# A two-layer decode step: one head's output weights on half of the DMA engines, scores on all 32 rows of a block, and three more filler matmuls

## The chip, the cores and the metric

The kernel runs on one core of one Trainium2 chip. The metric is device time in microseconds. Before the change the runs took 711.59, 712.06 and 712.72 us; their median, 712.06 us, is the time before.

## The reference, cut to what matters

Four tokens (B = 4, one position each, D = 640) go through attention, an MLP, the same attention and the same MLP again. The weights and the caches of the two attention layers are the same arrays, and so are those of the two MLPs. Everything is float32.

```python
x = x + A(layernorm(x));  x = x + M(layernorm(x))     # round one
x = x + A(layernorm(x));  x = x + M(layernorm(x))     # round two

def A(x):                       # 32 heads of 128, the last 1024 positions of the cache
    q = (x @ wq).reshape(B, 1, 32, 128).transpose(0, 2, 1, 3)
    p = softmax(einsum("bhqd,bhkd->bhqk", q, k) * 128 ** -0.5)
    o = einsum("bhqk,bhkd->bhqd", p, v)
    return o.transpose(0, 2, 1, 3).reshape(B, 1, 4096) @ wo

def M(x):                       # D -> 1728 -> D
    return relu(x @ w1) @ w2
```

Keys and values differ per batch entry and per head, so almost nothing that is loaded is used more than four times, and one round reads about 150 MB.

## The kernel before, in words

**Data.** For each head a record of 9,472 columns on 128 rows lies in HBM: the head's part of wq (5 blocks of 128 columns), its keys for 4 batch entries (4,096 columns), its values (4,096 columns) and its part of wo (640 columns; a row is one of the head's 128 dimensions). On the chip, `store` has room for some five records, `ring` has 4,320 columns and `kept` the tail of one record. The MLP's weights lie in a second array and come through `ring` and a spare part of `store`.

**Rounds and heads.** A loop `for r in range(2)` (line 501) makes the two rounds; r is 0 in round one and 1 in round two. Round one takes heads 0 to 31. Its last five records stay in `store`, and round two begins with them. Inside a round the heads are pipelined (lines 514 to 539): in step n PE makes the scores of head n+1, the values of head n, and the query of head n+2, and then projects head n's output.

One head's work is:

- `query` (line 385): 5 matmuls of 128 by 128 weights give q for four batch entries; DVE scales it into `qT`.
- `scores` (line 398): for each half of the positions and each batch entry b one matmul of 512 columns. The weights are q of entry b, repeated; the result goes to rows 32b and following of a PSUM tile `sc_ps`. The repetition is 4, so rows 32b to 32b+3 hold the same scores and the other 28 rows of the block hold what was there before.
- `softmax` (line 413): DVE takes the maximum over each row, ACT the exponential over all 128 rows with the sum of each row to `tot`.
- `weights` (line 421): DVE brings the sum of each block's first row to all its 32 rows (a transpose of 32 columns to `spread`), takes the reciprocal, and multiplies it with the mask `of_batch` into a factor `mrt` for each row and batch entry. Then it transposes the exponentials in blocks of 32 by 32 and multiplies them by `mrt` into `wT`, from which PE reads them as weights.
- `values` (line 434): 8 matmuls; `picks` (line 444): DVE masks and sums the result; `output_T` (line 449): PE turns it, ACT copies it to `oTs`; `project` (line 454): 4 matmuls add the head's contribution to `acc`.

A float32 matmul stands in the profile as two instructions, so the 8 matmuls of a head's scores are 16 lines of PE.

**Late heads.** In round one the last six heads' wo pieces come after the keys and values of all heads, and are used at the round's end (lines 555 to 562).

**Order of the work.** Every engine runs its instructions in the order in which the program is written (class `InOrder`, line 88). All loads are issued by the queue of SP. They stand in a list `items` in a fixed order; `pump` (line 278) issues the next one as soon as its place on the chip is free, and never one ahead of another. `done` (line 300) tells that a piece has been used for the last time. `cols` (line 293) finds the columns of a loaded piece.

**Fillers.** `busy` (line 350) is a matmul whose result nobody reads; it keeps PE at work in places where it would wait. Four of them stand at the end of each round ahead of the last head's query (line 524).

**Who waits for whom at the end of round one.** The query of the last head waits for its record. The values of the last two heads wait for theirs, and the projections for the late wo pieces. Then the MLP starts with the weights that have come into `ring`, and each piece that it has used lets SP issue a further one, first of the MLP and then of round two's heads.

Of the kernel before, what the change touches and what calls it, by code (L numbers as in the profile page):

```python
# [32 lines left out]
F32 = mybir.dt.float32  # L33
AF = mybir.ActivationFunctionType
OP = mybir.AluOpType
# [3 lines left out]
P = 128  # L39
B, D, H, DH, W, FF = 4, 640, 32, 128, 1024, 1728  # L40
NB = 4
FD = D // NB
# [4 lines left out]
WQ, K, V, WO = 0, D, D + 4 * W, D + 8 * W  # L47
REC = 2 * D + 8 * W
# [11 lines left out]
KEPT = WO - 4 * 512  # L60
# [18 lines left out]
LATE = 6  # L79
# [2 lines left out]
FIVE = [REC + 6272, 2 * REC - 3072, 2 * REC - 3200]  # L82
LAST_FIVE = [REC + 4736, 2 * REC - 4736, REC, REC]
THREE = [REC + HALF, REC + HALF]
GROUPS = [{h: FIVE for h in range(0, 25, 5)}, {6: THREE, 9: FIVE, 14: FIVE, 19: LAST_FIVE}]


# [19 lines left out]


@with_exitstack
def decode_kernel(ctx: ExitStack, tc: tile.TileContext, xf, rec, wm, out):  # L110
    nc = tc.nc
    pe, dve, act, pool, sp = (InOrder(tc, e) for e in (nc.tensor, nc.vector, nc.scalar, nc.gpsimd, nc.sync))
    sb = ctx.enter_context(tc.tile_pool(name="sb", bufs=1))
# [4 lines left out]
    wT = scratch[:, :128].rearrange("p (i c j) -> p i c j", i=2, c=16)  # L118
# [4 lines left out]
    spread = scratch[:, 256:288]  # L123
    hT = scratch.rearrange("p (m j) -> p m j", j=32)
    oTs = sb.tile([P, LATE, B], F32, name="oTs")
    qT = sb.tile([P, B], F32, name="qT")
    of_batch = sb.tile([P, B], F32, name="of_batch")
    of_block = sb.tile([P, 4], F32, name="of_block")
    rows = sb.tile([P, 2 * B], F32, name="rows")
    pick, rrow = rows[:, :B], rows[:, B:]  # L130
    mrt = sb.tile([P, B], F32, name="mrt")
    small = sb.tile([P, 14], F32, name="small")
    nmax, rtot, rstd, eps, eps_dh, ones, unused, sums, tot0, tot1 = (small[:, i:i + 1] for i in range(10))
    squares = small[:, 10:]
    tot = [tot0, tot1]
    store = sb.tile([P, FIRST + NS * REC], F32, name="store")
    kept = sb.tile([P, REC - KEPT], F32, name="kept")
    ring = sb.tile([P, RING], F32, name="ring")

    sc_ps = [ps.tile([P, W], F32, name=f"sc_ps{i}") for i in range(2)]  # L140
    t_ps = ps.tile([P, 512], F32, name="t_ps")
    o_ps = ps.tile([P, 512], F32, name="o_ps")
    acc = ps.tile([P, 512], F32, name="acc")
# [30 lines left out]
    LAST = H - NS  # L174


    def home(h, r):

        if r:
            return FIRST + (h if h >= LAST else h - 6 + LAST) % NS * REC  # L180
        return (0 if h < NS else FIRST) + h % NS * REC

    items = []
# [4 lines left out]
    buffers = {"store": store, "ring": ring, "kept": kept}  # L188

    def load(src, lo, hi, buf, col, parts):  # L190
        items.append((src[:, lo:hi], buf, col, hi - lo, parts))

    def place(buf, col):
        return ("store", spare + FROM + col) if buf == "spare" else (buf, col)
# [6 lines left out]
    def run(r, lo, hi, buf, col):  # L201
        parts = [(("rec", r, h), max(lo - h * REC, 0), min(hi - h * REC, REC), col + max(h * REC - lo, 0))
                 for h in range(lo // REC, (hi - 1) // REC + 1)]
        load(rec, lo, hi, buf, col, parts)

    def piece(r, h, lo, hi, buf="store", col=None):
        run(r, h * REC + lo, h * REC + hi, buf, home(h, r) + lo if col is None else col)


    def group(r, h, sizes):  # L210
# [21 lines left out]
    for h in hs[:-3]:  # L232
        if h in GROUPS[0]:
            group(0, h, GROUPS[0][h])
        if h >= 25:
            piece(0, h, 0, KEPT if h == LAST - 1 else WO if h >= H - LATE else REC)
        if h == LAST - 1:
            piece(0, h, KEPT, WO, "kept", 0)
    ending(0, hs, True)
# [16 lines left out]
    c, end = new[1] * REC, new[6] * REC  # L256
    for buf, lo, hi in places:
        if lo == old[1]:
            piece(1, new[0], WO, REC, buf, lo)
        elif c < end:  # L260
            cut = max(x for x in cuts if x <= min(end, c + hi - lo))
            run(1, c, cut, buf, lo)
            c = cut
# [14 lines left out]
    def pump():  # L278

        while items:  # L280
            src, buf, col, n, parts = items[0]
            if any(b == buf and x < col + n and col < y for b, x, y in live):
                return
            sp.dma_start(buffers[buf][:, col:col + n], src)
            live.append((buf, col, col + n))
            for key, lo, hi, c in parts:
                at.setdefault(key, []).append((lo, hi, buf, c))
            items.pop(0)
# [1 line left out]
    def pieces(key):  # L290
        return at[key if key in at else (key[0], 0) + key[2:]]

    def cols(key, lo, n):

        for x, y, buf, col in pieces(key):
            if x <= lo and lo + n <= y:
                return buffers[buf][:, col + lo - x:col + lo - x + n]
        raise KeyError((key, lo, n))

    def done(key, lo, hi):  # L300

        if key[0] == "rec" and key[1] == 0 and key[2] >= LAST:
            return
        if key == ("rec", 0, 0):
            lo = max(lo, FIRST)
        for x, y, buf, col in pieces(key):
            free(buf, col + max(lo, x) - x, col + min(hi, y) - x)
        pump()
# [89 lines left out]
    def scores(r, h, s, first=False):  # L398
        key = ("rec", r, h)
        for i in range(2):  # L400
            for b in range(B):
                pe.matmul(sc_ps[s][32 * b:32 * b + 4, 512 * i:512 * i + 512], qT[:, b:b + 1].to_broadcast([P, 4]),
                          cols(key, K + 512 * (B * i + b), 512), start=True, stop=True)
            done(key, K + VH * i, K + VH * i + VH)
            if first and i == 0:
                if r:
                    unpark(0)
                deviation(eps_dh, float(DH), True)
                act.activation(unused, eps, AF.Exp)
                if r:  # L410
                    unpark(1)
# [8 lines left out]

    def weights(s, parts=((0, 2),)):
        if parts[0][0] == 0:

            dve.transpose(spread, tot[s].to_broadcast([P, 32]))
            dve.reciprocal(rtot, spread[:, 0:1])
            dve.tensor_scalar(mrt, of_batch, rtot, None, op0=OP.mult)
        for i, j in parts:
            w = sc_ps[s][:, 512 * i:512 * j]
            dve.transpose(w, w)
            dve.tensor_tensor(wT[:, i:j].rearrange("p i c j -> p (i c) j"),  # L430
                              w.rearrange("p (c j) -> p c j", j=32)[:, :, :B],
                              mrt.unsqueeze(1).to_broadcast([P, 16 * (j - i), B]), op=OP.mult)

    def values(r, h, last=False, fill=(0, 0)):
        key = ("rec", r, h)
# [10 lines left out]
        dve.tensor_tensor(o, o, of_block.unsqueeze(2).to_broadcast([P, 4, DH]), op=OP.mult)  # L446
        dve.tensor_reduce(on[last], o.rearrange("p c d -> p d c"), op=OP.add, axis=AX.X)

    def output_T(i, last=False, to=None):
        to = outs[last][:, :B] if to is None else to  # L450
        pe.matmul(to, on[last], pick, start=True, stop=True)
        act.copy(oTs[:, i], to)

    def project(r, h, i, end):
        key = ("rec", r, h)
        for n in range(NB):
            pe.matmul(acc[32 * n:32 * n + B, :FD], oTs[:, i], cols(key, WO + n * FD, FD),
                      start=False, stop=end, skip_group_check=True)
        done(key, WO, REC)
# [41 lines left out]
    for r in range(2):  # L501
        hs = order[r]
        late = LATE if r == 0 else 2
        center(384 * r, 128)
        query(r, hs[0], 0, True)
        if r:
            busy(192, warm)
        scores(r, hs[0], 0, True)
        softmax(0, (r, hs[1], 1))
        if r:  # L510
            unpark(2)
            unpark(3)
        weights(0, ((0, 1), (1, 2)))
        for n, h in enumerate(hs[:-2]):
            i = n - (H - late)
            s = (n + 1) % 2
            scores(r, hs[n + 1], s)
            if r and not n:
                busy()
            softmax(s)  # L520
            end = n == H - 3
            values(r, h)
            if end:
                for _ in range(4):
                    busy()
            picks(0)
            query(r, hs[n + 2], n + 2)
            if end:
                scores(r, hs[-1], 1)
                weights(s, ((0, 1),))  # L530
            if r and n < NS - 2:
                busy(320, sc_ps[n % 2])
            output_T(max(i, 0), to=None if r and not n else t_ps[:, :B])
            if r and not n:
                unpark(4)
            if i < 0:
                project(r, h, 0, False)
            if not end:
                weights(s)
        softmax(1)  # L540
        if not r:
            park(0)
            park(1)
        weights(0, ((1, 2),))
        values(r, hs[-2], 0, (0, 1))
        weights(1, ((0, 1), (1, 2)))
        picks(0)
        values(r, hs[-1], 1)
        if not r:
            park(2)  # L550
        output_T(late - 2)
        if not r:
            park(3)
        picks(1)
        for i in range(late - 3) if late > 2 else (0,):
            project(r, hs[H - late + i], i, False)
        if late == 2:
            busy()
        output_T(late - 1, True)
        dve.memset(pad, 0.0)  # L560
        for i in (late - 3, late - 1, late - 2) if late > 2 else (1,):
            project(r, hs[H - late + i], i, i == late - 2 or late == 2)
        center(256, 328)
        mlp(r)
# [39 lines left out]
```

## Time and profile before

| what | value |
|---|---|
| median of three runs | 712.06 us (711.59 to 712.72) |
| the profiled execution, first to last instruction | 710.7 us |
| TensorE busy | 502.4 us, 71% |
| VectorE busy | 317.4 us, 45% |
| ScalarE busy | 99.6 us, 14% |
| read from HBM | 301.34 MB |
| mean rate of all transfers | 425 GB/s |
| mean granted TensorE clock | 0.824 |

The profile is of one execution. Its own time is known as the span from its first to its last instruction, 710.7 us; the timed runs have 1.3 us more in the median, which lies ahead of the first or behind the last instruction.

How to read it: an engine's busy time says little here unless one asks for the stretch of the span. The page has a row of the DMA engines' busy share in 40 slices. The chain of waits goes back from the last instruction to whatever released each step; a step that begins with "DMA" counts from the issue of a transfer to its landing, so it holds the time in which the transfer stood behind others. A transfer has landed when the slowest of the 16 DMA engines has done its part. In the tables of instructions every operation has line 102 or 99, the helper that records it, so operations are told apart by the tiles that they write and read: `sc_ps<-store,qT` are scores, `o_ps<-store,scratch` are values, `misc<-xT,store` queries, `acc<-store,oTs` projections, `acc<-kept,small` fillers, `scratch<-sc_ps,mrt` the multiplication in `weights`, `mrt<-of_batch,small` and `scratch<-small` its factor and its transpose of 32 columns.

### The profile page before, as it was taken

The numbers are of one execution on the slowest core, as the hardware profiler recorded it, in microseconds if no ns is written. First come the engines' busy times: TensorE is split into PE (matmuls) and PEld (weight loads), VectorE is DVE, ScalarE is ACT, GpSimd is POOL, SyncE is SP. The second block draws the span as 40 slices with busy tenths as digits, with TensorE's granted clock in tenths as the row PEclk, the third lists the DMA queues.
The fourth block names the chain that finished last, engine by engine and source line by source line (L and its number), as shares of the span: only waits on it lengthen the run. The fifth ranks groups of instructions, "written<-read, shape, count | busy, mean of one in ns | idle before, by whom it ended". The sixth has DMA issues, their size and how long they took to land.

```text
span 710.7 us, 8613 instructions
## 1 busy us (share of the span) xinstructions
PE 502.4 (71%) x3722; PEld 199.5 (28%) x3722; DVE 317.4 (45%) x645; ACT 99.6 (14%) x210; POOL 1.1 (0%) x9
## 2 busy tenths in 40 slices
PE   0675677576677686868788998756577685695985
PEld 0331322231332222333223333322222231332322
DVE  2252344253443353546541866625244253453661
ACT  0210111011010110111130421201010011011120
POOL 0000000000000000000000000000000000000000
PEclk9987787677676778788999999969687677788899
DMA  9999999999999999999999999999999999999996
GB/s 397 436 416 451 422 435 447 417 435 447 420 429 451 427 429 420 425 444 420 426 404 396 411 425 434 447 429 436 442 431 433 434 428 436 430 427 421 430 427 281
DMA packets 12741, 301.97 MB, mean 425 GB/s; under 512 B 1424, under 2 KB 1568, under 8 KB 4640
## 3 DMA queue, kind: packets, MB, share of 16 engines
q1 hardware_dynamic: 12672, 301.42, 98.9%
q8 instruction: 29, 0.48, 0.2%
q14 instruction: 8, 0.07, 0.0%
q10 hardware_dynamic: 32, 0.01, 0.0%
HBM read 301.34 MB, written 0.08 MB: 424 GB/s over the span
## 4 chain that ended last, share of the span: by engine, by line
DMA 68%; PE 25%; DVE 4%; another core or an unknown queue 1%; ACT 1%; issue 1%; SPq 0%; ACTq 0%
DMA store<-rec 60%; PE sc_ps L102 10%; PE o_ps L102 7%; DMA store<-wm 5%; PE acc L102 3%; PE misc L102 3%; DMA ring<-wm 3%; DVE scratch L102 2%; DVE o_ps L102 2%; PE t_ps L102 2%; ACT oTs L102 1%; DVE small L102 0%; ACT sc_ps L102 0%; DVE sc_ps L102 0%
## 5 line engine op out<-in xcount | busy, mean ns | idle before, releaser
L102 PE MATMUL sc_ps<-store,qT 128*4 128x512 f32 x1024 | 193.7, 852 | 37.8 <-DMA store<-rec 36.4
L102 PE MATMUL misc<-xT,store 128*128 128x4 f32 x620 | 92.8, 276 | 100.6 <-DMA store<-rec 100.0
L102 DVE TENSOR_REDUCE small<-sc_ps 128x1 f32<-128x1024 f32 x64 | 78.4, 1224 | 157.9 <-PE sc_ps L102 157.8
L102 PE MATMUL o_ps<-store,scratch 128*16 128x512 f32 x960 | 142.1, 667 | 4.6 <-DVE scratch L102 2.9
L102 PEld LDWEIGHTS misc<-xT,store 128*128 128x128 f32 x620 | 87.4, 221 | 156.2 <-DMA store<-rec 123.1
L102 ACT ACTIVATE sc_ps<-sc_ps,small 128x1024 f32<-128x1024 f32 x64 | 69.8, 1091 | 325.2 <-DVE small L102 325.2
L102 DVE STREAM_TRANSPOSE sc_ps<-sc_ps 128x1024 f32<-128x1024 f32 (+1 forms) x70 | 81.7, 1167 | 0.1
L102 PEld LDWEIGHTS sc_ps<-store,qT 128*4 128x4 f32 x1024 | 32.7, 107 | 121.2 <-issue 66.4
L102 PEld LDWEIGHTS o_ps<-store,scratch 128*16 128x16 f32 x960 | 32.3, 114 | 118.6 <-issue 100.7
L102 DVE TENSOR_TENSOR o_ps<-o_ps,of_block 128x512 f32<-128x512 f32 x62 | 43.4, 699 | 45.9 <-PE o_ps L102 45.8
L102 DVE TENSOR_TENSOR qT<-misc,rows 128x4 f32<-128x4 f32 x61 | 9.5, 156 | 112.7 <-PE misc L102 112.6
L102 PE MATMUL acc<-store,oTs 128*4 128x160 f32 x488 | 34.6, 365 | 17.1 <-ACT oTs L102 17.0
L102 DVE TENSOR_REDUCE scratch<-o_ps 128x128 f32<-128x512 f32 x62 | 42.9, 692 | 2.1
L102 ACT COPY oTs<-t_ps 128x4 f32<-128x4 f32 x59 | 9.6, 162 | 204.5 <-PE t_ps L102 204.5
L102 PE MATMUL t_ps<-rows,scratch 128*128 128x4 f32 x118 | 25.5, 286 | 11.4 <-DVE scratch L102 10.9
L102 PEld LDWEIGHTS t_ps<-rows,scratch 128*128 128x128 f32 x118 | 21.4, 226 | 17.9 <-DVE scratch L102 14.2
L102 DVE TENSOR_TENSOR scratch<-sc_ps,mrt 128x128 f32<-128x128 f32 (+1 forms) x70 | 19.6, 280 | 2.7
L102 PE MATMUL acc<-kept,small 128*1 128x328 f32 (+2 forms) x54 | 17.4, 428 | 0.0
L99 PE MATMUL acc<-scratch,ring 128*128 128x160 f32 x2 | 0.9, 540 | 22.2 <-DMA scratch<-xf 22.2
L102 DVE TENSOR_SCALAR mrt<-of_batch,small 128x4 f32<-128x4 f32 x64 | 14.7, 230 | 2.2
L102 DVE STREAM_TRANSPOSE scratch<-small 128x32 f32<-128x32 f32 x64 | 12.9, 202 | 2.4 <-ACT sc_ps L102 2.4
L102 PEld LDWEIGHTS acc<-store,oTs 128*4 128x4 f32 x488 | 6.9, 84 | 22.9 <-ACT oTs L102 21.9
(84 smaller groups left out, 123.1 us busy)
## 6 DMA issues: line engine op xcount, KB each, us to landing
store<-rec SPq DMA_DIRECT2D x14, 7872.0 KB, 28.9
store<-rec SPq DMA_DIRECT2D x7, 7936.0 KB, 30.9
store<-rec SPq DMA_DIRECT2D x4, 7104.0 KB
store<-rec SPq DMA_DIRECT2D x11, 2368.0 KB, 34.8
store<-rec SPq DMA_DIRECT2D x3, 4736.0 KB, 27.2
store<-rec SPq DMA_DIRECT2D x2, 4416.0 KB, 28.3
store<-rec SPq DMA_DIRECT2D x5, 1024.0 KB, 20.2
store<-rec SPq DMA_DIRECT2D x1, 4160.0 KB, 20.7
```

The source lines that it names most:

```text
L99: r = build(*args, **kwargs)
L102: r = build(*args, **kwargs)
```

## The change

Four things change.

1. The wo piece of head 25 (`SPLIT`) comes in another way in round one. A host array `halves` holds it with rows 0 to 63 and rows 64 to 127 of the piece side by side, as 64 rows of 1,280 columns, in two groups of 32 rows; each group is laid out as 8 times 4 rows, with one unused row behind every four, so that the two dimensions stay apart. Two transfers bring it to rows 0 to 31 and 32 to 63 of `ring`, columns 128 to 1,407, right behind the rest of head 25's record. In round two head 25 is loaded as before.
2. Head 25's projection in round one takes its two halves: 8 matmuls over 64 rows each. For that ACT makes a second copy, of rows 64 to 127 of the head's output, to a tile `upper` on rows 0 to 63.
3. The scores' weights repeat q 32 times, so all 32 rows of a block hold the same scores, and `tot` has the same sum in all of them. The transpose to `spread` and the product into `mrt` go; one instruction multiplies the exponentials by the reciprocal, a scalar for each row, and by the mask.
4. In round one seven fillers instead of four stand ahead of the last head's query.

```diff
+SPLIT = 25
+HALVES_AT = 128
...
+    upper = sb.tile([64, B], F32, name="upper")
...
     def load(src, lo, hi, buf, col, parts):
-        items.append((src[:, lo:hi], buf, col, hi - lo, parts))
+        items.append(([(src[:, lo:hi], 0, P)], buf, col, hi - lo, parts))
...
+    def halves_of(r):
+        shares = [(halves[q][:, :4], 32 * q, 32) for q in range(2)]
+        items.append((shares, "ring", HALVES_AT, 2 * D, [(("halves", r), 0, 2 * D, HALVES_AT)]))
...
         if h >= 25:
-            piece(0, h, 0, KEPT if h == LAST - 1 else WO if h >= H - LATE else REC)
+            piece(0, h, 0, KEPT if h == LAST - 1 else WO if h >= H - LATE or h == SPLIT else REC)
+            if h == SPLIT:
+                halves_of(0)
...
         while items:
-            src, buf, col, n, parts = items[0]
+            shares, buf, col, n, parts = items[0]
             if any(b == buf and x < col + n and col < y for b, x, y in live):
                 return
-            sp.dma_start(buffers[buf][:, col:col + n], src)
+            for src, row, rows in shares:
+                sp.dma_start(buffers[buf][row:row + rows, col:col + n], src)
...
-                pe.matmul(sc_ps[s][32 * b:32 * b + 4, 512 * i:512 * i + 512], qT[:, b:b + 1].to_broadcast([P, 4]),
+                pe.matmul(sc_ps[s][32 * b:32 * b + 32, 512 * i:512 * i + 512], qT[:, b:b + 1].to_broadcast([P, 32]),
                           cols(key, K + 512 * (B * i + b), 512), start=True, stop=True)
...
     def weights(s, parts=((0, 2),)):
         if parts[0][0] == 0:
-            dve.transpose(spread, tot[s].to_broadcast([P, 32]))
-            dve.reciprocal(rtot, spread[:, 0:1])
-            dve.tensor_scalar(mrt, of_batch, rtot, None, op0=OP.mult)
+            dve.reciprocal(rtot, tot[s])
         for i, j in parts:
             w = sc_ps[s][:, 512 * i:512 * j]
             dve.transpose(w, w)
-            dve.tensor_tensor(wT[:, i:j].rearrange("p i c j -> p (i c) j"),
-                              w.rearrange("p (c j) -> p c j", j=32)[:, :, :B],
-                              mrt.unsqueeze(1).to_broadcast([P, 16 * (j - i), B]), op=OP.mult)
+            dve.scalar_tensor_tensor(wT[:, i:j].rearrange("p i c j -> p (i c) j"),
+                                     w.rearrange("p (c j) -> p c j", j=32)[:, :, :B], rtot,
+                                     of_batch.unsqueeze(1).to_broadcast([P, 16 * (j - i), B]), op0=OP.mult,
+                                     op1=OP.mult)
...
-    def output_T(i, last=False, to=None):
+    def output_T(i, last=False, to=None, split=False):
         to = outs[last][:, :B] if to is None else to
         pe.matmul(to, on[last], pick, start=True, stop=True)
         act.copy(oTs[:, i], to)
+        if split:
+            act.copy(upper, to[64:])
 
     def project(r, h, i, end):
         key = ("rec", r, h)
+        if (r, h) == (0, SPLIT):
+            key = ("halves", r)
+            for half, o in ((0, oTs[:64, i]), (1, upper)):
+                for n in range(NB):
+                    pe.matmul(acc[32 * n:32 * n + B, :FD], o, cols(key, half * D + n * FD, FD, 64), start=False,
+                              stop=False, skip_group_check=True)
+            done(key, 0, 2 * D)
+            return
...
             if end:
-                for _ in range(4):
+                for _ in range(4 if r else 7):
                     busy()
...
+    halves = np.zeros((2, 8, 5, 2 * D), k.dtype)
+    halves[:, :, :4] = np.concatenate([rec[SPLIT, :64, WO:], rec[SPLIT, 64:, WO:]], 1).reshape(2, 8, 4, 2 * D)
```

More of the change, by code (lines that the diff above doesn't have):

```diff
@@ L109, in decode_kernel @@
 @with_exitstack
-def decode_kernel(ctx: ExitStack, tc: tile.TileContext, xf, rec, wm, out):
+def decode_kernel(ctx: ExitStack, tc: tile.TileContext, xf, rec, halves, wm, out):
     nc = tc.nc
@@ L291, in pieces, with cols @@
         return at[key if key in at else (key[0], 0) + key[2:]]
-    def cols(key, lo, n):
+    def cols(key, lo, n, rows=P):
         for x, y, buf, col in pieces(key):
             if x <= lo and lo + n <= y:
-                return buffers[buf][:, col + lo - x:col + lo - x + n]
+                return buffers[buf][:rows, col + lo - x:col + lo - x + n]
         raise KeyError((key, lo, n))
@@ L532, in decode_kernel @@
                 busy(320, sc_ps[n % 2])
-            output_T(max(i, 0), to=None if r and not n else t_ps[:, :B])
+            output_T(max(i, 0), to=None if r and not n else t_ps[:, :B], split=(r, h) == (0, SPLIT))
             if r and not n:
@@ L592 @@
         "rec": rec.transpose(1, 0, 2).reshape(P, H * REC),
+        "halves": halves,
         "wm": np.concatenate([block_rows(np.asarray(B_w1)).transpose(1, 0, 2).reshape(P, KB * FF), *tiles], 1),
```

## The prediction

> **What bounds the kernel now.** I read the span, the page's slices and its queues first. One core streams its weights and caches once per round, and all 16 DMA engines (lanes, below) are at work in every slice but the last.
>
> ```profile
> core 0: 710.7 us, clock 0.824
> DMA  9999999999999999999999999999999999999996
> ...
> q1 hardware_dynamic: 12672, 301.42, 98.9%
> q8 instruction: 29, 0.48, 0.2%
> q14 instruction: 8, 0.07, 0.0%
> ```
>
> The kernel's own transfers (q1) fill 98.9% of 16 lanes over the span. At most 1.1% of 710.7 us, 7.8 us, could go by keeping lanes busier, and the start and the tail are in that. What takes lane time beside q1 is instruction fetch: 29 packets on q8 and 8 on q14. Then I asked for stages (columns: stretch, its length, busy time of PE, PEld, DVE, ACT, POOL, granted clock, DMA share, GB/s), the end of the stream last.
>
> ```profile
> 355.00:411.00 56.00, 47.83 (x462) 17.83 (x458) 27.61 (x67) 13.26 (x26) 0.00 (x0) 1.00 1.01 404
> 392.00:398.00 6.00, 5.08 (x41) 1.88 (x44) 5.43 (x13) 3.06 (x6) 0.00 (x0) 1.00 0.97 383
> 412.00:460.00 48.00, 43.12 (x360) 17.42 (x359) 32.47 (x63) 9.42 (x22) 0.00 (x0) 0.89 1.02 435
> 702.00:707.00 5.00, 3.11 (x88) 2.11 (x76) 0.00 (x0) 0.00 (x0) 0.00 (x0) 1.00 0.52 213
> 706.00:707.00 1.00, 1.00 (x33) 0.70 (x24) 0.00 (x0) 0.00 (x0) 0.00 (x0) 1.00 0.10 41
> ```
>
> With the lanes full the flow is 435 GB/s. Between the rounds, 355 to 411, it is 404: 56 us x (1 - 404/435) = 4.0 us are lost there, mostly in short packets, since the share stays near 1.00. At the end the lanes do not finish together. Of the 5 us from 702 to 707 the lanes are busy 0.52, and in the last of them 0.10, so the mean lane is done near 704.6 and the last near 707. **The last landing, which the program waits for, belongs to a late lane.** What makes lanes late is seen in a window of 2 us around one fetch:
>
> ```profile
> q8 instruction: 1, 0.02, 2.9%
> ```
>
> 2.9% of 16 x 2.0 us is 0.93 us on one lane; 29 of them are 27 lane-us. Last the chain of waits from the end of round one to round two's second head:
>
> ```profile
> 325.79 33.97 DMA store<-rec
> 359.77 8.88 DMA ring<-wm
> ...
> 394.91 0.23 DVE scratch L102
> ...
> 395.16 0.17 DVE small L102
> ...
> 395.58 0.64 DVE sc_ps L102
> ...
> 398.61 1.21 PE misc L102 x10
> ```
>
> From 325.79 to 368.65 the chain is landings, and they are the last lane's, since a wait ends with the last. Further on landings and compute alternate, and from 394.91 to 398.61 it is DVE and PE. The transfers issued as the first head's values end (398.61) fill the queue again, and from 412 on the lanes never run dry (1.02, 435 GB/s), so the end follows from when they got going and from each lane's own load.
>
> **The change, part by part.** The sum is made against the profiled execution, 710.7 us of span; the runs' median, 712.06, is 1.3 us above that, outside the first and last instruction, and the difference that I find is applied to the median.
>
> *(a) Head 25's wo by eight lanes.* The same bytes come in two transfers of 32 rows, 5 KB a row, instead of 128 rows of 2.5 KB.
>
> ```profile
> store<-rec SPq DMA_DIRECT2D x7, 320.0 KB, 19.2
> ```
>
> 320 KB at 435 GB/s are 0.75 us on each of 16 lanes, or 1.51 us on eight. So eight lanes gain 0.75 us and eight lose 0.75. If the relieved lanes are those that carry the fetches, the last lane at the end of round one lands up to 0.75 us earlier; if they are the others, up to 0.75 later. No view prints lanes, so both ends stay in the range. Fetches make lanes late by 0.93 us a time and some lanes of the other half are late too (the eight fetches of q14, the first transfers), and those become the last ones: I take -0.5 us, two thirds of the full gain. SP issues two more transfers of the same queue, ahead of heads 26 and later; its backlog there is 30 us deep (the chain's 33.97 us from issue to landing), so a later issue costs nothing. The piece lies in the ring until head 25 is projected, six heads before the MLP's weights need the place.
>
> [...]
>
> *(b) Weights' factors in one instruction.* Of the DVE's work per head a transpose, a tensor_scalar and the hand-over between them go.
>
> ```profile
> L102 DVE TENSOR_TENSOR scratch<-sc_ps,mrt 128x64 f32<-128x64 f32 x2 | 0.5, 225 | 0.1
> L102 DVE TENSOR_SCALAR mrt<-of_batch,small 128x4 f32<-128x4 f32 x1 | 0.2, 229 | 0.0
> L102 DVE STREAM_TRANSPOSE scratch<-small 128x32 f32<-128x32 f32 x1 | 0.2, 215 | 0.2 <-ACT sc_ps L102 0.2
> L102 DVE TENSOR_TENSOR qT<-acc,rows 128x4 f32<-128x4 f32 x1 | 0.2, 161 | 0.0
> L102 DVE SCALAR_TENSOR_TENSOR scratch<-scratch,rows 128x32 f32<-128x32 f32 x1 | 0.2, 193 | 0.0
> L102 DVE SCALAR_TENSOR_TENSOR scratch<-scratch,rows 128x28 f32<-128x28 f32 x1 | 0.2, 189 | 0.0
> ```
>
> On the chain 394.91 to 395.58 shrinks to one reciprocal of 0.17: -0.5 us. The multiply gets a per-row scalar: 229 against 161 on four columns says +0.07, so -0.43. In the other 63 heads this lies under PE's work or a landing and is worth nothing; DVE is busy 32.47 of 48 us even where PE is densest. Of the 0.43 only what lanes really waited for at 398 counts: their share is 0.97 in 392 to 398, so 0.03 x 6 = 0.18 us a lane. I take -0.2, between 0 and -0.43.
>
> [...]
>
> *(c) Scores on 32 rows.* As many matmuls over as many columns, but weights of 32 columns instead of 4.
>
> ```profile
> L102 PEld LDWEIGHTS misc<-xT,store 128*128 128x128 f32 x30 | 3.6, 191 | 2.6 <-issue 2.6
> L102 PEld LDWEIGHTS o_ps<-store,scratch 128*16 128x16 f32 x56 | 1.4, 96 | 5.2 <-DVE scratch L102 3.1 <-issue 2.2
> L102 PEld LDWEIGHTS sc_ps<-store,qT 128*4 128x4 f32 x48 | 1.3, 87 | 2.1 <-issue 1.9
> ...
> L102 PE MATMUL o_ps<-store,scratch 128*16 128x512 f32 x52 | 6.5, 594 | 0.6 <-DVE scratch L102 0.6
> L102 PE MATMUL sc_ps<-store,qT 128*4 128x512 f32 x48 | 5.7, 592 | 0.0
> ```
>
> These groups are of the PE-bound stretch 396 to 416. A load of 4 columns takes 87 ns, of 16 columns 96, of 128 columns 191: 0.8 ns a column, so 32 columns should take some 110. Matmuls behind 4 and 16 columns take 592 and 594 ns: the loads hide under running matmuls. I take 0; the far end is the 104 ns between 4 and 128 columns on each of 16 loads a head, 1.7 us. DVE and ACT already work on all 128 rows, so they cost the same.
>
> *(d) Three more fillers before round one's last query.*
>
> ```profile
> 346.26 2.37 PE L102 MATMUL acc<-kept,small 128*1 128x328 f32 x8
> 350.05 1.28 PE L102 MATMUL misc<-xT,store 128*128 128x4 f32 x10 [1.42 <-DMA store<-rec]
> 351.58 3.48 PE L102 MATMUL sc_ps<-store,qT 128*4 128x512 f32 x16 [0.25 <-DVE qT L102]
> 680.82 1.90 PE L102 MATMUL sc_ps<-store,qT 128*4 128x512 f32 x16 [0.25 <-DVE qT L102]
> ```
>
> Four fillers are eight instructions here, 2.37 us or 0.3 each, so three more are 6 x 0.3 = 1.8 us. They lie in the 1.42 us in which PE waits for the last query's columns; 0.4 us stick out, 0.9 if that landing comes 0.5 earlier by (a). Behind them wait the query, the scores and all of the last head. Against that, these scores run 3.48 us here, 1.90 in the same place of round two: the clock fell, and if the fillers hold it the scores end about 1.6 us sooner. Neither reaches the end as long as the landings at 359.76 and 368.65 are waited for anyway. I take 0, with +0.9 if that cover is gone and the clock still falls, and -1.6 + 0.4 = -1.2 if compute sets this stretch and the clock is held.
>
> *(e) Head 25's projection* becomes eight matmuls of 64 rows plus one ACT copy; as wide a projection now takes 0.71 us.
>
> ```profile
> 320.62 0.71 PE acc L102 x8
> ```
>
> Twice as many matmuls make +0.7 us at most, behind which the next scores on PE and then SP's issue at 325.79 wait. That transfer lands 33.97 us after its issue because it queues behind others, and this backlog hides it: 0, and +0.7 without the backlog.
>
> Sum: -0.5 - 0.2 = **-0.7 us**, 712.06 to **711.4**.
>
> **Rivals.** (1) *The transfer is spread over 16 lanes after all*, or the chain ignores the relief: only (b) remains, 711.9. [...] (2) *The wrong lanes are relieved*: +0.75 - 0.2, 712.6. (3) *Round one's end is bound by compute*: the kept clock's 1.2 us reach the end and so does all of (b), 1.2 + 0.5 + 0.43 = 2.1, 709.9. For it: 351.58 with 3.48 us; against it the chain, which is landings from 325.79 on. (4) *Slower: wide weights come out exposed.* Place: the scores of round two's first two heads, both ahead of 398.61, where nothing is buffered; 2 x 1.7 = 3.4 us, less the 0.7 gained: 714.8. It decides once the loads add over 1 us a head; the rows of 592 and 594 ns speak against it.
>
> **How the numbers follow.** Within 0.2% (1.4 us, about what a measurement of this kernel tells from no change) means 710.6 to 713.5. Chances: forecast 0.66, (1) 0.12, (2) 0.07, (3) 0.10, (4) 0.05. Of the forecast a tenth may spill below 710.6 and a fiftieth above 713.5, since which lane is last can change by a fetch of 0.93 us. Faster: 0.10 + 0.07 = 0.17. Slower: 0.05 + 0.02 = 0.07. Same: 0.76. The range goes from (3), 709.9, to just past (2), 712.9, and leaves out (4) and the far side of (3).
>
> **What would show it.** (a): the chain's landing at 359.76 comes about 0.5 us earlier; the windows of the last 5 us look the same. (b): 394.91 to 395.58 becomes 0.2 us, and the multiply of 64 columns takes under 0.3 us. (c): score matmuls stay near 592 ns in 396 to 416 with loads near 110 ns. (d): the scores at 351.6 take 1.9 us and the chain still runs over landings. The forecast is wrong if the chain after 325 runs over PE, if DMA shares fall under 0.95 between 392 and 412, or if the last 5 us stretch.

## The result, and the profile after

The changed kernel takes 716.0 us (median of 6 runs, 714.95 to 717.93), the kernel before 712.26 (6 runs beside them): a ratio of 1.0055, 95% interval 1.0041 to 1.0069. It is slower by 3.7 us where 0.7 us less was forecast. The profiled execution has 713.4 us of span against 710.7.

The page of the changed kernel first, its span, DMA slices and queues:

```profile
core 0: 713.4 us, clock 0.816
DMA  9999999999999999999999999999999999999996
...
q1 hardware_dynamic: 12752, 301.42, 98.9%
q8 instruction: 29, 0.48, 0.3%
q14 instruction: 7, 0.06, 0.0%
```

The lanes carry the same 301.42 MB at the same share of a longer span: they are as full as before and finish later. So the same bytes have taken longer. The instruction fetches too: the same 29 packets have gone from 0.2 to 0.3%. The 80 packets more are the 64 rows of the halves and, for each of the two transfers, a closing packet of 4 bytes on each of its eight lanes (1,424 packets of 4 bytes where the kernel before has 1,408, 16 for each of the queue's 88 transfers). The stages of the same execution (columns as in the prediction: stretch, length, PE, PEld, DVE, ACT, POOL, granted clock, DMA share, GB/s):

```profile
20.00:280.00 260.00, 180.59 (x1194) 76.59 (x1195) 99.86 (x171) 34.40 (x72) 0.00 (x0) 0.77 1.00 432
300.00:355.00 55.00, 43.68 (x314) 17.81 (x306) 26.16 (x43) 8.36 (x19) 0.00 (x0) 0.85 1.00 425
355.00:411.00 56.00, 46.59 (x448) 17.83 (x452) 24.90 (x59) 12.89 (x24) 0.00 (x0) 1.00 1.01 400
702.00:707.00 5.00, 1.80 (x44) 1.21 (x44) 0.00 (x0) 0.00 (x0) 0.00 (x0) 1.00 0.91 378
706.00:707.00 1.00, 0.00 (x0) 0.00 (x0) 0.00 (x0) 0.00 (x0) 0.00 (x0) 1.00 0.66 266
```

And two of these of the kernel before, which the prediction did not show:

```profile
20.00:280.00 260.00, 181.32 (x1196) 73.50 (x1196) 108.76 (x217) 34.39 (x72) 0.00 (x0) 0.78 1.00 433
300.00:355.00 55.00, 42.42 (x313) 16.53 (x313) 29.55 (x58) 8.20 (x18) 0.00 (x0) 0.88 1.00 429
```

Share 1.00 in both, 425 GB/s after and 429 before from 300 to 355: the lanes are never idle and move 1% less. In 702 to 707 they are busy 0.91, not 0.52. The mean lane, not only the last one, is done about 2 us later. The chain of waits after, from the end of round one on:

```profile
327.69 32.90 DMA store<-rec
360.60 9.11 DMA ring<-wm
...
370.72 6.78 DMA ring<-wm
...
394.95 1.30 ACT sc_ps L104 x2
...
396.44 0.64 DVE sc_ps L104
397.10 0.29 DVE scratch L104
...
399.58 1.21 PE misc L104 x10
```

It runs over the same landings, 0.83 us later at 360.60 (359.77 before), and is 0.97 us late at the query of round two's third head (399.58, 398.61 before). The rest of the loss comes after that, in round two, which has no part of the change but the scores and the factors.

### The profile page after: what moved, and what is told of

It is laid out like the page before. It is cut to its first block, busy times and chain, and to the rows that moved or that the text cites. A ratio compares the mean times of both kernels' runs of the same rounds, so it can differ in the third digit from the quotient of the medians.

```text
span 713.4 us, 8519 instructions
## 1 busy us (share of the span) xinstructions
PE 504.4 (71%) x3736; PEld 210.8 (30%) x3736; DVE 293.3 (41%) x517; ACT 99.7 (14%) x211; POOL 1.1 (0%) x9
## 3 DMA queue, kind: packets, MB, share of 16 engines
q1 hardware_dynamic: 12752, 301.42, 98.9%
## 4 chain that ended last, share of the span: by engine, by line
DMA 70%; PE 23%; DVE 3%; another core or an unknown queue 1%; ACT 1%; issue 1%; SPq 0%; ACTq 0%
DMA store<-rec 62%; PE sc_ps L104 9%; PE o_ps L104 7%; DMA store<-wm 5%; DMA ring<-wm 3%; PE acc L104 3%; PE misc L104 3%; DVE scratch L104 2%; DVE o_ps L104 1%; PE t_ps L104 1%; ACT oTs L104 1%; DVE small L104 0%; ACT sc_ps L104 0%; DVE sc_ps L104 0%
## 5 line engine op out<-in xcount | busy, mean ns | idle before, releaser
L104 PE MATMUL sc_ps<-store,qT 128*32 128x512 f32 x1024 | 190.5, 837 | 43.7 <-DMA store<-rec 42.3
L104 PE MATMUL misc<-xT,store 128*128 128x4 f32 x620 | 94.9, 280 | 95.6 <-DMA store<-rec 95.4
L104 PE MATMUL o_ps<-store,scratch 128*16 128x512 f32 x960 | 144.8, 680 | 2.0 <-DVE small L104 1.1
L104 PEld LDWEIGHTS misc<-xT,store 128*128 128x128 f32 x620 | 89.5, 225 | 151.8 <-DMA store<-rec 118.4
L104 PEld LDWEIGHTS sc_ps<-store,qT 128*32 128x32 f32 x1024 | 40.9, 138 | 117.1 <-issue 58.9
L104 PE MATMUL acc<-store,oTs 128*4 128x160 f32 x480 | 32.5, 351 | 17.6 <-ACT oTs L104 16.7
L104 DVE SCALAR_TENSOR_TENSOR scratch<-sc_ps,small,of_batch 128x128 f32<-128x128 f32 (+1 forms) x70 | 23.8, 340 | 2.7
L104 PE MATMUL acc<-kept,small 128*1 128x328 f32 (+2 forms) x60 | 19.1, 429 | 0.0
L104 ACT ACTIVATION_READ_ACCUMULATOR sc_ps<-sc_ps,small 128x1 f32 x64 | 12.3, 193 | 0.0
```

Of the source, the lines that this page charges most:

```text
L104: r = build(*args, **kwargs)
```

## Experiments

### One part at a time

Four kernels, each with one piece of the change on top of the kernel before: the split with its projection; the scores with the factors; the fillers; and the array of halves passed in but never read.

```diff
 e1  + the array halves, its two transfers, the tile upper, the projection over 64 rows
 e2  - qT[:, b:b + 1].to_broadcast([P, 4])     + ...([P, 32]);  weights(): reciprocal, scalar_tensor_tensor
 e3  - for _ in range(4):                      + for _ in range(4 if r else 7):
 e4  - decode_kernel(ctx, tc, xf, rec, wm, out)  + decode_kernel(ctx, tc, xf, rec, halves, wm, out)
```

> The kernel before with part (a) and the projection (e) alone: head 25's wo comes in two transfers of 32 rows from an array of its own. Theory 'lanes' (the eight lanes that take the pieces include late ones, so the last lane gets later): this run alone brings most of the +3.7 us, 714 to 716, and the landing at the end of round one (359.77 before) comes 0.5 to 1.0 us later. Theory 'placement' (a further array moves the others in device memory, and every packet gets a few ns longer): 714 to 716 too, but the kernel that only passes the array shows the same. Theory 'wide weights' (scores on 32 rows slow the lanes): 712 within 0.7.

> The kernel before with parts (b) and (c) alone: weights of 32 columns for the scores, and the weights' factors in one instruction. Theory 'wide weights' (loads of 32 columns, or what they read, slow PE or the lanes): 714 to 716, loads of 128*32 near 138 ns as in the changed kernel. Theories 'lanes' and 'placement': 711.6 to 712.2, since (b) takes 0.2 to 0.4 us off the stretch 394.91 to 395.58 and nothing else changes.

> The kernel before with part (d) alone: seven fillers instead of four ahead of round one's last query. All theories: 712.1 within 0.7, since the landings set that stretch; if the last query is pushed back onto the chain, up to 0.9 us more. The scores behind it, 3.48 us before, take 1.9 us if the fillers keep the clock.

> The kernel before, with the array of head 25's halves passed in and not read; the computation is that of before. Theory 'placement': 713 to 714.5, and the shares of the DMA engines rise for the same bytes. Theories 'lanes' and 'wide weights': 712.1 within 0.5.

Measured, against 712.17 us (35 runs): split 715.91 (ratio 1.0041, 1.0017 to 1.0064), scores 712.18 (0.9983, 0.9960 to 1.0006), fillers 712.91 (0.9994, 0.9968 to 1.0020), array 712.25 (0.9988, 0.9964 to 1.0013). By the medians the split alone has the whole loss, 3.7 us. The ratios lie some 0.1% lower than the medians have it, and their intervals are wide: two of the 35 runs beside took 719.4 and 719.5 us. The array in device memory and the wide weights are out. The split's stages:

```profile
300.00:355.00 55.00, 40.96 (x322) 16.76 (x322) 30.48 (x61) 8.53 (x20) 0.00 (x0) 0.88 1.00 425
702.00:707.00 5.00, 1.98 (x45) 1.21 (x44) 0.66 (x3) 0.00 (x0) 0.00 (x0) 1.00 0.90 377
```

The same 425 and 0.90 as the changed kernel. Theory "lanes" would have a late end too, but it can't say why the mean lane is late. The single packets of the traces do: each is one row, and for a size nearly all of them take the same time. A count over them (median and 90th percentile in ns, from 44 us on; last column: time above the line 9.2 ns + 18.82 ns per 512 bytes, in us per lane, for 44 to 300, 300 to 355 and 411 to the end; nearly all rows of the kernel before lie within 2 ns of that line):

```
                 2560 B      8192 B      18944 B     62976 B       above the line
before           102, 102    309, 309    705, 705    2324, 2324    0.39  0.00  0.32
changed          102, 111    313, 320    708, 715    2327, 2334    0.90  0.37  1.47
e1 split         102, 111    313, 320    708, 715    2327, 2334    0.90  0.36  1.54
e2 scores        102, 102    309, 309    705, 705    2324, 2324    0.44  0.00  0.24
e4 array         102, 102    309, 309    705, 705    2324, 2324    0.43  0.01  0.32
```

**Rows of every size take longer, by 0 to 4 ns in the median and 9 to 11 at the 90th percentile, long before the halves are issued at 263 us.** In the three stretches that is 0.51 + 0.37 + 1.15 = 2.0 us a lane. A cost for each row, early and late, is not that of one transfer. Something that the split changes for the whole program is left, and the edit has one: it allocates a tile, `upper`, ahead of the buffers. Tiles are placed one after the other in steps of 32 bytes, so `store`, `kept` and `ring` begin at byte 3104, 201248 and 212000 of a row, 32 further than before.

### Where the buffers begin

```diff
 e5, the changed kernel:
-    upper = sb.tile([64, B], F32, name="upper")                 (behind qT)
+    upper = sb.tile([64, B], F32, name="upper")                 (behind ring)
 e6, the kernel before:
+    unused_tile = sb.tile([64, B], F32, name="unused_tile")     (behind qT)
 e7, the split alone:
-    upper = sb.tile([64, B], F32, name="upper")
+    upper = sb.tile([64, 4 * B], F32, name="upper")[:, :B]
 e8: e2 and e3 together
```

> The changed kernel, with its new 16-byte tile 'upper' allocated behind the buffers instead of ahead of them. Tiles are placed in steps of 32 bytes, so in the changed kernel the buffers store, kept and ring begin at byte 3104, 201248 and 212000 of a row, 32 past a multiple of 64; here they begin at 3072, 201216 and 211968 as in the kernel before. Theory 'placement in SBUF' (rows that begin 32 bytes off a multiple of 64 make each transfer a few ns longer, 800 rows a lane, 2 to 3 us in all): 711.5 to 713, and the DMA share from 702 to 707 falls back from 0.91 towards 0.5. Theory 'lanes' (the eight lanes of the pieces include late ones): 715 to 716 as the changed kernel.

> The kernel before with one more tile of 16 bytes a row ahead of the buffers, never used, so that they begin 32 bytes further. Nothing else changes: no part of the change is in it. Theory 'placement in SBUF': 714 to 715.5, all of the loss. Theory 'lanes': 712.2, as before.

> The split alone (715.9 in the run of parts (a) and (e)), with the new tile 64 bytes wide instead of 16, so the buffers begin 64 bytes further than before, at a multiple of 64 again. Theory 'placement in SBUF', if it is the 32 bytes: 711.5 to 713, what the split itself is worth; if any other address costs, 715.9 stays. Theory 'lanes': 715.9 stays.

> The changed kernel without the split: scores on 32 rows, one instruction for the factors, seven fillers; buffers where they were before. Both theories: 711.5 to 712.3; a theory by which the parts hurt only together would have 714 or more.

Measured, against 712.2 us (23 runs): e5 712.62 (1.0004, 0.9993 to 1.0015), **e6 715.64 (1.0042, 1.0030 to 1.0054)**, e7 715.65 (1.0047, 1.0034 to 1.0060), e8 712.23 (0.9999, 0.9990 to 1.0007). A tile that nobody uses costs the kernel before 3.4 us, and the loss of the changed kernel, 3.7 us, falls to 0.4 when its tile stands elsewhere. Theory "lanes" falls. So does the first form of theory "placement in SBUF": 64 bytes are no better than 32. Stages of e6:

```profile
300.00:355.00 55.00, 41.66 (x302) 17.09 (x294) 28.48 (x56) 8.04 (x17) 0.00 (x0) 0.86 1.00 426
702.00:707.00 5.00, 3.92 (x60) 1.63 (x49) 1.34 (x5) 0.00 (x0) 0.00 (x0) 1.00 0.92 383
```

and of e5:

```profile
300.00:355.00 55.00, 43.60 (x336) 18.36 (x336) 28.77 (x46) 9.03 (x21) 0.00 (x0) 0.91 1.00 428
702.00:707.00 5.00, 2.75 (x68) 1.68 (x68) 0.33 (x1) 0.00 (x0) 0.00 (x0) 1.00 0.26 104
```

The flow from 300 to 355 is the safer sign of the two. The profile of e5 is of its fastest execution, 710.6 us, and its last 5 us are emptier for that. The profile of e4 is of its slowest, 715.11 us, and its lanes are busy to the end although its rows are not longer (0.01 us a lane above the line from 300 to 355); there the time from 355 to 411 went up, by the same count from 1.93 us a lane (before) to 3.25:

```profile
300.00:355.00 55.00, 42.53 (x313) 16.92 (x313) 29.64 (x62) 8.21 (x18) 0.00 (x0) 0.85 1.00 429
702.00:707.00 5.00, 2.99 (x49) 1.48 (x47) 1.34 (x5) 0.00 (x0) 0.00 (x0) 1.00 0.83 347
```

### From which power of two on

Three orders of the tiles of the kernel before, with nothing added. Of its transfers into these buffers all begin at a multiple of 256 bytes from the buffers' start, most at one of 512.

```diff
 e9   xT and scratch allocated behind ring:                            store at  512
 e10  oTs, qT, of_batch, of_block, rows and mrt behind ring:           store at 2816 = 11 x 256
 e11  xT behind ring:                                                  store at 2432 = 19 x 128
```

> The kernel before with two small tiles, xT and scratch, allocated behind the buffers: store, kept and ring begin at 512, 198656 and 209408, all multiples of 512 as in the kernel before (3072, 201216, 211968), but everything lies elsewhere. Theory 'alignment' (the rows of the stream must begin at a multiple of 512, or of some smaller power): 712.2 within 0.6. Theory 'place' (what costs is a small tile at another place, or the buffers at any other address): 714.5 to 716 as in the two runs with 32 and 64 bytes.

> The kernel before with six small tiles (256 bytes together) behind the buffers, which begin at 2816, 200960 and 211712: multiples of 256, not of 512. Theory 'alignment to 512': 714.5 to 716. Theory 'alignment to 256 or less': 712.2 within 0.6; for it speaks that the kernel before already writes six of its 92 transfers to multiples of 256 alone, and its rows of 12800 bytes there take 479 ns, no more than the others by size.

> The kernel before with xT alone behind the buffers, which begin at 2432, 200576 and 211328: multiples of 128, not of 256. Theory 'alignment to 256 or more': 714.5 to 716. Theory 'alignment to 128': 712.2 within 0.6. With the two runs beside it this says from which power of two on the rows cost nothing.

Measured, against 712.35 us (22 runs): e9 712.12 (0.9993, 0.9984 to 1.0003), e10 712.72 (1.0005, 0.9996 to 1.0013), e11 715.21 (1.0040, 1.0027 to 1.0053). With the packets of all six places:

```
store begins at           62976 B       above the line       us
3072 (before), 512, 2816  2324, 2324    0.4  0.00  0.3       712.1 to 712.7
2432 = 128 off            2326, 2332    0.76 0.28 1.22       715.2
3136 =  64 off (e7)       2326, 2333    0.77 0.29 1.28       715.7
3104 =  32 off            2327, 2334    0.89 0.36 1.51       715.6
```

Theory "place" falls with e9 and e10, where small tiles and buffers have moved and nothing is lost. **With the buffers at 512, 2816 or 3072, all multiples of 256 bytes, rows cost nothing more (2324 ns for 62,976 bytes); at 32, 64 or 128 bytes off, a row of that size takes 2 to 3 ns more in the median and 8 to 10 at the 90th percentile.** Not every row pays: from 300 to 355 us 93% of them lie over 1 ns above the line at 32 off (e6), 85% at 64 and 63% at 128, none in the kernel before. The stretch from 300 to 355 and the last 5 us, of e10 and then of e11:

```profile
300.00:355.00 55.00, 39.46 (x308) 16.12 (x304) 30.10 (x58) 8.43 (x19) 0.00 (x0) 0.91 1.00 429
702.00:707.00 5.00, 3.09 (x87) 2.15 (x83) 0.00 (x0) 0.00 (x0) 0.00 (x0) 1.00 0.57 234
```

```profile
300.00:355.00 55.00, 41.39 (x298) 17.11 (x294) 28.41 (x56) 8.05 (x17) 0.00 (x0) 0.86 1.00 426
702.00:707.00 5.00, 2.42 (x44) 1.40 (x44) 0.00 (x0) 0.00 (x0) 0.00 (x0) 0.77 0.79 328
```

At 128 bytes off a lane loses a little less than at 32, 0.28 against 0.36 us from 300 to 355 and 1.22 against 1.51 from 411 on, since fewer rows pay. Why the step is 256 bytes no run shows.

### What the relief of eight lanes is worth

With the buffers in place, the split can be judged by itself. Two kernels take e5 and read the 64 rows in one transfer by all 16 lanes; in e13 a row of 5 KB stands empty behind every four of the array, as it does in the changed kernel. e14 is e5 again, beside e13.

```diff
 e12, e13, from e5:
-        shares = [(halves[q][:, :4], 32 * q, 32) for q in range(2)]
+        shares = [(halves[:, :], 0, 64)]         (e12: array of 64 rows, packed)
+        shares = [(halves[:, :4], 0, 64)]        (e13: array of 16 x 5 rows, four of five used)
```

> The changed kernel with 'upper' behind the buffers, and head 25's wo read as one transfer of 64 rows of 5 KB by all 16 lanes, in place of two of 32 rows by eight. All else is as in the run with 'upper' behind (712.6, profiled run 708.9 of span). Theory 'the relief works' (the eight lanes without the pieces carry most fetches and land 0.5 earlier at the last): 0.5 slower than that run, 713.1, and the landing that ends round one's stream 0.4 to 0.5 us later. Theory 'the relief is worth nothing': 712.3 to 712.6.

> As the run with 64 rows by all 16 lanes (714.7), but with a row of 5 KB left empty behind every four rows of the array in device memory, as the changed kernel has it: each lane's four rows then begin 25600 bytes after the last lane's, not 20480. 'upper' lies behind the buffers. Theory 'layout in device memory' (what slowed 293 to 298 to 263 GB/s was how 16 lanes read the packed array): 293 to 298 at 430 GB/s or more again, and 712.2 to 713.1. Theory 'sixteen lanes' (any transfer of 64 rows by 16 lanes does it): 714.7 stays. Between 712.2 and 713.1 the relief of the eight lanes is told: 0.5 over the run beside it if it works, the same if it is worth nothing.

> The changed kernel with 'upper' behind the buffers, the two transfers by eight lanes, beside the 16-lane one on the same chip: 712.0 to 712.9 by either theory. If the relief works it is 0.5 faster than the run with 16 lanes and padding, and the landing that ends round one's stream comes 0.4 to 0.5 us earlier than there; if not, the two are the same.

Measured: e12 714.72 (1.0030, 1.0019 to 1.0042, against 712.35), e13 713.62 (1.0015, 1.0003 to 1.0026, against 712.53), e14 712.73 (1.0003, 0.9993 to 1.0014, against 712.53). The stretch in which the 64 rows arrive, of e5, e12 and e13 in turn:

```profile
293.00:298.00 5.00, 5.00 (x40) 1.16 (x28) 1.84 (x3) 0.49 (x1) 0.00 (x0) 0.66 1.03 438
```

```profile
293.00:298.00 5.00, 5.00 (x34) 1.03 (x24) 1.68 (x3) 0.45 (x1) 0.00 (x0) 0.66 0.97 263
```

```profile
293.00:298.00 5.00, 5.00 (x40) 1.24 (x32) 1.89 (x3) 0.04 (x1) 0.00 (x0) 0.67 1.02 308
```

Read by 16 lanes at once, the small array slows them all: 5 us x (1 - 263/438) = 2.0 us are lost in e12 and 1.5 in e13. In e12 rows of 5120 bytes take 196 to 409 ns there, by eight lanes 196 each, and the rows of other arrays that start in this stretch take 0.5 us more in the median. So these two can't be the undisturbed 16-lane form that was wanted, and the empty rows explain a part at most. For the relief e5 and e14 against the kernel before are left: by their ratios +0.3 and +0.2 us, with 0.8 us to either side, and e8, without the split, stands at -0.1 with 0.6. It brings no gain that can be told, and the packets suggest why. Lanes are told apart here by following each packet to the one that starts at its end, which is a reconstruction; the numbers of the lanes are arbitrary:

```
               lanes of the first eight 16 KB fetches (p: a lane       last lane behind the mean
               of the two pieces), then of the ninth, about 265 us     as round one's rec ends
before         9  15  6  14  2  13  7  12, then 9                      2.05 us
e5             7  8  14  9  13  11  4p  12p, then 7                    1.58 us
e14            1p  10  9  11  14  12  15  5p, then 1p                  2.23 us
```

As far as they were followed, fetches go around eight lanes, and two of the eight carry the pieces too. In e5 the lane with two fetches by 265 us is a relieved one, and the last lane is 0.47 us nearer to the mean; in e14 it carries the pieces, and is 0.18 us farther. Where the round begins differs between these two executions, so the relief would be a gain in some and a loss in others; two executions can't say how often.

## Why the prediction was wrong, point by point

**The step that failed is the sum, "-0.5 - 0.2": it takes for granted, as (a) does with "The same bytes come in two transfers of 32 rows", that a byte of the stream costs what it did before.** I priced what the edit transfers and computes, and put what it allocates at nothing. The projection (e) was priced with its ACT copy, but the tile that the copy writes moved three buffers by 32 bytes, and so made most rows of a stream that fills 98.9% of the lanes some 3 to 10 ns longer. That term is +3.4 us (e6). With 712.2 for the kernel before and +0.4 for the aligned change (the medians of e5) it gives 716.0, the measured median; to the tenth that is luck, since the six runs spread from 714.95 to 717.93. About 2.0 us of the 3.4 are the longer rows outside 355 to 411; fetches of 1054 ns in place of 965 (means of the 29 in the changed kernel and in the one before) add, by an estimate, some 0.3 on a lane with three or four. What the rest is made of isn't shown: from 355 to 411 the packets lie 2.4 us a lane above the line in the changed kernel, but between 1.0 (e5) and 3.3 (e4) in kernels whose rows are in place, so one profile can't tell. Of the signs that the forecast named for its being wrong one came, "if the last 5 us stretch"; the chain still ran over landings, and the lanes' share from 392 to 398 was 0.98.

**(a)** Its sign was left to chance: -0.5 was taken, and the whole change with aligned buffers stands at +0.2 and +0.3. The intervals end at -0.5 us, so that a gain of 0.7 for the whole change is excluded; (a) by itself is known no better. One reading was wrong, with no effect on the sum: in the kernel before, head 25's wo were not 128 rows of 2.5 KB but the ends of its record's 128 rows of 37,888 bytes; the rows of 2.5 KB in the line shown are those of the late heads. And a fetch costs its lane more than the 0.93 us that were taken: by the same reconstruction 0.9 us pass in the kernel before between two rows of the lane, and the row behind takes 0.5 us more. Part of the mechanism was there: eight lanes take the pieces, and in one execution the last lane gained 0.47. What did not hold is the choice in "If the relieved lanes are those that carry the fetches": of the eight lanes with the fetches six are relieved and two are not, and which of them comes last differs between the two executions. Of rival (1) the first half is refuted: the 64 rows came on eight lanes, eight on each. The closing packets show it too, eight for each of the two transfers and sixteen for each of SP's others. No run had shown an eight-lane transfer when the forecast took 0.75 us a lane for it; and that the fetches of q14 would make lanes of the other half late as well, the ground for taking two thirds of that, was an estimate which no trace shows. The other half of rival (1), a chain that ignores the relief, can't be told from what e5 and e14 show. Rival (2), wrong lanes, has the right direction in e14, and its 712.6 is by chance what e5 and e14 take; by e6 nearly all of the loss comes without it.

**(b)** On the chain the saving came as worked out. From ACT's end (396.25) to the transposition (396.44) there are 0.19 us after and were 0.70 (394.88 to 395.58). The multiplication, whole span, after and before:

```profile
L104 DVE SCALAR_TENSOR_TENSOR scratch<-sc_ps,small,of_batch 128x128 f32<-128x128 f32 x58 | 20.4, 351 | 2.0
L104 DVE SCALAR_TENSOR_TENSOR scratch<-sc_ps,small,of_batch 128x64 f32<-128x64 f32 x12 | 3.4, 284 | 0.7
```

```profile
L102 DVE TENSOR_TENSOR scratch<-sc_ps,mrt 128x128 f32<-128x128 f32 x58 | 16.9, 292 | 2.0
L102 DVE TENSOR_TENSOR scratch<-sc_ps,mrt 128x64 f32<-128x64 f32 x12 | 2.7, 225 | 0.7
```

+59 ns at either size, where 0.07 us were taken; 64 more columns cost 67 ns by either instruction, so the new one runs at no lower rate than the old. Of the 0.2 us that were to reach the end none can be told in e2 or e8; with 0.6 us to either side in e8 that neither confirms nor refutes it.

**(c)** Right. Loads of 32 columns take 110 ns where PE sets the pace, as worked out, and hide, with 592 ns a matmul as before:

```profile
L104 PEld LDWEIGHTS sc_ps<-store,qT 128*32 128x32 f32 x48 | 1.6, 110 | 1.9 <-issue 1.8
...
L104 PE MATMUL sc_ps<-store,qT 128*32 128x512 f32 x52 | 6.3, 592 | 0.0
```

Rival (4) is refuted by e2 and e8.

**(d)** Right at the end of the kernel, and (3) is refuted, since its 709.9 lies far outside e8. The fillers fill PE's wait, the scores behind them take 1.92 us as forecast, and nothing of it that can be told reaches the end (e8), since the landing at 360.60 is waited for anyway:

```profile
346.83 4.02 PE L104 MATMUL acc<-kept,small 128*1 128x328 f32 x14
350.79 1.28 PE L104 MATMUL misc<-xT,store 128*128 128x4 f32 x10
352.32 1.92 PE L104 MATMUL sc_ps<-store,qT 128*32 128x512 f32 x16 [0.26 <-DVE qT L104]
```

That the fillers keep the clock is likely, but not shown by one profile. From 351 to 355 the granted clock was 0.57 before and 1.00 after, and all seven profiles with seven fillers have these scores at 1.90 or 1.92 us. Of the nine with four fillers seven have 2.69 to 3.53, and two, e1 and e10, have 1.90 behind as long a wait; in e1:

```profile
350.78 1.28 PE L104 MATMUL misc<-xT,store 128*128 128x4 f32 x10 [1.50 <-DMA store<-rec]
352.31 1.90 PE L104 MATMUL sc_ps<-store,qT 128*4 128x512 f32 x16 [0.25 <-DVE qT L104]
```

**(e)** As priced: the projection takes 1.25 us in place of 0.71 on the chain, ahead of a landing that comes 33 us after its issue.

```profile
321.35 1.25 PE acc L104 x16
```

No version tried beats the kernel before: the intervals of e2, e8 and e9, the nearest, all hold 1.

## What to carry to other kernels

When an edit allocates, work out where every buffer behind it then begins, and put small tiles behind the buffers that a stream fills; here 256 bytes was the step to keep, with nothing lost that can be told in e9 and e10 and 3.4 us in e6. A loss with the DMA share unchanged and GB/s down by 1% in the full stretches was here a loss per row, and the times of single packets show it at once, where waits and chains only pass it on. A late end by itself does not say so, as e4 shows. Shift one lane against another only where it is known which lane comes last, and that it is the same in every execution.

## What the runs showed of the hardware

Not expected: in the six places tried a row cost more where the buffers began off a multiple of 256 bytes in SBUF (2326 or 2327 ns in the median against 2324, for 62,976 bytes), and not in every phase. From 20 to 44 us rows of misplaced buffers cost nothing more (0.00 us a lane above the line, as in all kernels); from then on more of them do. Over 1 ns above the line are, in e6, 56% of the rows from 44 to 100 us, 95% from 100 to 300, 43% from 355 to 411 and 87% after that; in the kernel before 21%, 4%, 5% and 1%. What must come together for it isn't shown. And 16 lanes that read 64 rows of 5 KB from 320 KB of device memory brought the whole stream to 263 GB/s (e12), rows of other arrays included; two transfers by eight lanes each did not (438, e5). With 5 KB left empty behind every four rows it was 308 (e13). Whether the closeness of the rows or their number at once does it wasn't tried, and no trace shows which rows a lane reads.
